# A fused attention and feed-forward kernel: a new order for its first two chunks, and another place in memory for the squares

## The chip, the cores and the metric

One core of a Trainium2 chip runs the whole program in one launch. The metric is device time in microseconds (us); lower is better. PE is TensorE (its matmuls), DVE VectorE, ACT ScalarE, POOL GpSimd, and SP the engine that issues the loads and stores.

## The reference

```python
# attention: 4 batches, 8 heads, 768 positions of 64; windows of 16, blocks of 32
k_sum = k.reshape(B, H, nb, block, D).max(axis=3)       # nb = 24 blocks
v_sum = v.reshape(B, H, nb, block, D).mean(axis=3)
scores_l = scale * q @ k.T, outside |i - j| < window: -1e9
scores_s = scale * einsum('bhsd,bhnd->bhsn', q, k_sum) + log(block)
a = softmax(concatenate([scores_l, scores_s], axis=-1))
attn = a @ concatenate([v, v_sum])                      # -> x, 3072 tokens x 512
# feed-forward: 512 -> 2048 -> 512
h = maximum(x @ w_in, 0.0)
out = h * h @ w_out
```

## The kernel before

The 3072 tokens are 24 tiles of 128 (6 to a batch) and 12 chunks of two tiles. For a tile, `scores` or `scores_kt` makes the scores on PE, `mask_max` (DVE) adds the mask and finds the maximum, `exponentials` (ACT) takes the exponential, `inverse` (DVE) and `norm` (mostly POOL) divide, `turn` (DVE) or `turn_pe` (PE) transposes, and `outputs` (PE) multiplies by the values. `high_x` (ACT) and `low_x` (DVE) split the result into a high and a low part, `xh` and `xl`, from the pool `work`.

The hidden 2048 is 16 slices f of 128. The first layer, `ffn1`, makes per slice 12 matmuls of 256 columns (4 pieces of the 512, each as xh by high weight, xh by low weight, xl by high weight): stationary are 128 columns of the weights `w_sb`, moving is `xh` or `xl`. `squares` takes the ReLU, the square and its high and low parts `gh` and `gl`. The second layer, `ffn2`, makes 6 matmuls of 512 columns per slice: stationary is `gh` or `gl`, moving is `w_sb`. All these operands are fp32r. In all there are 2304 matmuls of the first layer (L390) and 1152 of the second (L434).

Weights arrive as 64-bit words and are split once, at the start, by six steps per slice: HI (`sign_w`, ACT), LO (`round_w`, ACT or DVE), SH (`shift_w`, DVE), AD (`add_w`, POOL), CA (`high_w`, ACT or DVE), SU (`low_w`, DVE or POOL). Slices 0 to 3 do it in halves (.1 is the first layer's, .2 the second's).

Two things set the order. Chunks 2 to 11 are a loop of eight slots (`slot`, `period`), in which attention for the next chunk is laid between. Chunks 0 and 1 with their attention, the split of the weights and all loads of batch 0 follow the list `START` (L42), a token for each step in the order in which every engine takes it: `L:x0` loads value tile 0, `KS` is a maximum of keys, `S` scores, `TT` `mask_max`, `E` `exponentials`, `NR` `inverse`, `N` `norm`, `T` a transpose on PE and `TC` its copy, `SV` and `VC` the value means and their copies, `PK` the copy of the key maxima, `O` `outputs`, `XH`/`XL` the split, `F1.u.j` and `F2.u.j` the two layers of unit u (two slices of one chunk), `RE SQ MU GL` the squares' steps, `EV` an eviction, `Z` zero matmuls that fill PE's time. A letter a, v or p at the end puts a step on ACT, DVE or POOL.

Loads go out on SP, in the list's order; a load whose buffer isn't free holds back those behind it. The means of values (`sum_v0`, L154) need all four `x` loads; `outputs` of tile 0 and 1 need the means. The mask comes with `consts` (L553).

The pool `const` is laid out in the order of its lines, then `big` (18 slots of 8192 bytes for weights), then `work`. Two unnamed tiles, `gap0` (L101, ahead of gh) and `gap` (L110), hold nothing.

Of the kernel before, what the change touches and what calls it, by code (L numbers as in the profile page):

```python
# [43 lines left out]
TT0.2 L:w0.1 TT0.0 L:q2 TT0.3 E0.2 S0.1=23 TT0.1 E0.3 E0.1 E0.0 TT0.6 TT0.4 S1.0=45 TT0.5 S1.1=45 TT0.7 L:w0.2 E0.4
SU2.1p HI0.1 NR0.0 LO0.1v TT1.0 S2.1=01 E0.7 E0.6 SH0.1 TT1.4 TT1.6 E0.5 N0.0p NR0.1 E1.0 S2.0=01 TT1.5 E1.6 L:w1.1
TT1.3 N0.1p T0.0=2 Z2 TT1.1 E1.4 L:q3 T0.1=3 Z3 L:k4 TT1.2 E1.5 TT1.7 LO1.1v E1.7 LO0.2v E1.3 E1.1 TT2.0 TT2.3 TT2.4
L:x0 NR1.1 E1.2 TC0.1a NR1.0 TT2.1 HI0.2 AD0.1 TT2.2 TC0.0v E2.2 L:q4 TT2.5 S3.0=45 TT2.7 HI1.1 N1.1p TT2.6 E2.0 SH0.2
N1.0p S3.1=45 L:x1 L:x3 E2.3 T1.1=3 Z1 E2.4 E2.1 T1.0=2 SH1.1 CA0.1v AD0.2 TC1.0a TT3.6 S4.0=01 TT3.0 E2.6 TT3.7 E3.7
TC1.1v E2.7 TT3.4 TT3.5 SV0 Z5 E2.5 L:x2 E3.6 NR2.0 TT3.1 CA1.1v TT3.3 NR2.1 SV1 TT3.2 S4.1=01 Z1 L:w3.1 E3.4 E3.3
VC0.3a AD1.1 VC0.2v VC0.1a VC0.0v VC1.2a L:w2.2 E3.5 N2.0p L:w3.2 L:w6 VC1.0v HI3.1 VC1.3v SU1.1p VC1.1v N2.1p O0=2  # L50
E3.2 L:w1.2 NR3.1 N3.1v O1=3 XH0 XH1 E3.1 PK5a XL0 XL1 LO3.1a L:w4 E3.0 SH3.1 T2.1=4 VX3v L:q5 CA3.1a T3.1=5 TC3.1a
T2.0=2 SU0.1p AD3.1 F1.0.0=3 F1.0.1 L:k5 NR3.0 TT4.5 TT4.6 TC2.0v CA0.2a TC2.1v HI2.2 F1.1.0=5 VX2a SU0.2v SH2.2 L:w11
HI1.2 RE0v TT4.7 N3.0p T3.0=2 SQ0 SU3.1p L:w7 MU0 LO1.2a SH1.2 CA1.2v CA2.2v O2=4 GL0v AD1.2 TC3.0a TT4.0 XH2 F1.1.1
LO3.2v SU1.2v HI3.2 O3=2 F2.0.0 L:w5 LO2.2v HI4 SH3.2 XL2 XH3 LO4a CA3.2a TT4.1 L:w8 F2.0.1 XL3 AD3.2 E4.0 E4.1 E4.6
S5.1=34 AD2.2 TT4.3 HI7 S5.0=34 TT4.2 HI5 SH4 SU2.2p F1.2.0=2 TT5.4 RE1v SQ1 TT4.4 AD4 L:k6 MU1 F1.2.1 RE2v CA4a TT5.1
L:q6 F1.3.0=0 TT5.7 SU3.2p MU2 F1.3.1 GL1v SU4v LO5a RE3a SQ2 SH5 F2.1.0 L:w9 GL2v TT5.6 F2.1.1 HI6 L:kw2 EV0.0v
F1.4.0=1 EV0.1a SQ3 E4.3 MU3 CA5a HI11 TT5.0 AD5 LO6a SH7 F2.2.0 LO7a LO9v SU5v CA7v SH6 F1.6.0=5 CA6a AD6 L:w10
F2.2.1 F1.4.1 GL3v RE4v HI8 E4.5 SU6v SH8 VT2 L:k7 HI9 L:w12 AD7 E5.0 HI10 L:w13 F2.3.0 TT5.3 KT2 SU7v LO8a F1.6.1
TT5.2 F1.7.0=2 AD8 SQ4 MU4 E5.7 F2.3.1 E4.4 E5.6 GL4v CA8a F1.5.0=0 TT5.5 F1.5.1 LO10a SH10 F2.4.0 F2.4.1 SU8v RE5a
F1.7.1 SQ5 SH9 SH11 HI12 E4.2 HI13 MU5 CA9a F1.12.0=1 RE6v AD9 F1.8.0=3 SQ6 CA11a GL5v MU6 AD10 L:kw3 E4.7 VT3 SU9v  # L60
F2.5.0 F2.5.1 SH13 CA10a NR4.1 RE7v EV1.0v F1.8.1 F1.12.1 E5.2 SU10v GL6p SH12 MU7 EV1.1v LO11a F1.9.0=4 L:w14
F1.13.0=0 RE8a LO12a F2.6.0 AD11 E5.1 F2.6.1 E5.3 HI14 SU11v NR4.0 N4.1p F1.9.1 SQ7 AD12 LO14a E5.4 KT3 MU8 F1.13.1
GL7v L:w15 F2.7.0 LO13a N4.0v SQ8 GL8v CA12a CA13a AD13 LO15a SH14 SU12v RE9a SU13p F2.7.1 E5.5 AD14 MU9 HI15 F2.8.0
F2.8.1 F1.14.0=5 L:kw0 TU4.2 F1.10.0=2 SQ9 F1.10.1 CA14a SH15 SU14v CA15a F1.11.0=3 KT0 AD15 GL9v SU15p F2.9.0 F2.9.1
RE10v SQ10 TU4.1 MU10 NR5.1 GL10v F1.11.1 RE11v SQ11 F2.10.0 MU11 VT0 GL11v F1.15.0=4 NR5.0 RE12a MU12 RE13v F2.10.1
N5.1p SQ12 MU13 F2.11.0 GL12v F2.11.1 EV2.0v L:kw1 F1.14.1 EV2.1v KT1 F1.15.1 L:q7 L:v4 N5.0p SQ13 PK6a GL13p RE15a
TU5.0 F2.12.0 RE14a TU4.0 MU14 TU5.2 S6.1=01 F2.12.1 F2.13.0 F2.13.1 SQ14 MU15 GL14p L:v5 O4=2 F2.14.0 TU5.1 S6.0=01
# [680 lines left out]
```

## Time and profile before

| | us |
|---|---|
| median of 3 runs (622.3 to 624.28) | 622.73 |
| the profiled execution, its own time | 622.01 |
| its span, first to last instruction | 619.9 |
| PE busy | 607.6 |
| DVE busy | 389.8 |
| ACT busy | 267.4 |
| POOL busy | 106.2 |

What lies between the span and the execution's own time is 2.1 us. A matmul's busy time is longer than the distance from its start to the next one's start, since matmuls overlap: for the pace of PE look at starts, not at durations. A time in brackets behind a row is idle time of the engine before it and what ended it.

### The profile page before, as it was taken

The page shows a single profiled execution, that of the slowest core. Times are in us where ns is not written, and L with a number is a line of the kernel's source. Part 1 is how long each engine was busy: PE and PEld are TensorE (multiplying, and loading weights), DVE is VectorE, ACT ScalarE, POOL GpSimd, SP SyncE. Part 2 cuts the span into 40 slices and gives each one's busy share as a digit, 9 for nine tenths or more (in the row PEclk, how much of TensorE's full clock was granted, in tenths as well). Part 3 has the DMA queues.
Part 4 walks back from the last instruction along what each step waited for, and adds up shares of the span by engine and source line. Part 5 has one row for each costly group of instructions (what it writes and reads, how often), then busy time and mean ns, then how long its engine had stood idle before and what let it go on. Part 6 is the DMA issues. An engine that isn't in the chain of part 4 may idle for free.

```text
span 619.9 us, 12969 instructions
## 1 busy us (share of the span) xinstructions
PE 607.6 (98%) x5253; PEld 546.5 (88%) x5253; DVE 389.8 (63%) x1063; ACT 267.4 (43%) x688; POOL 106.2 (17%) x98
## 2 busy tenths in 40 slices
...
GB/s 329 410 413 336 52 136 52 153 193 30 1 9 264 2 2 220 2 2 221 1 2 188 86 1 126 97 1 76 95 2 38 133 1 1 87 1 1 35 1 34
DMA packets 21643, 59.41 MB, mean 96 GB/s; under 512 B 2256, under 2 KB 2256, under 8 KB 20048
## 3 DMA queue, kind: packets, MB, share of 16 engines
...
q14 instruction: 18, 0.15, 0.1%
...
## 4 chain that ended last, share of the span: by engine, by line
PE 93%; DVE 2%; ACT 2%; DMA 2%; SPq 1%; issue 0%; POOL 0%; DVEq 0%; POOLq 0%
PE o_ps L434 42%; PE ph L390 39%; PE s_ps L390 5%; PE ph L360 3%; PE s_ps L277 3%; DMA consts_sb<-in_consts 1%; ACT e_sb L313 1%; DVE w_sb L262 1%; PE s_ps L360 1%; DMA kv<-in_kt 0%; PE o_ps L159 0%; DVE v_sb L126 0%; SPq L180 0%; DVE ksum L188 0%; PE s_ps L339 0%
## 5 line engine op out<-in xcount | busy, mean ns | idle before, releaser
L390 PE MATMUL ph<-xh,w_sb 128*128 128x256 f32 x1360 | 246.8, 282 | 0.5 <-DVE xl L377 0.5
L434 PE MATMUL o_ps<-w_sb,gh 128*128 128x512 f32 x768 | 239.0, 392 | 0.0
L390 PEld LDWEIGHTS ph<-xh,w_sb 128*128 128x128 f32 x1360 | 213.4, 188 | 8.6 <-issue 1.4
L390 PE MATMUL ph<-xl,w_sb 128*128 128x256 f32 x680 | 190.5, 280 | 0.0
L434 PEld LDWEIGHTS o_ps<-w_sb,gh 128*128 128x128 f32 x768 | 137.6, 188 | 25.2 <-issue 0.2
L409 DVE TENSOR_TENSOR ph<-ph,r 128x512 f32<-128x512 f32 x83 | 58.1, 699 | 151.7 <-ACT r L398 150.9
L434 PE MATMUL o_ps<-w_sb,gl 128*128 128x512 f32 x384 | 151.2, 394 | 0.0
L398 ACT ACTIVATE r<-ph 128x512 f32<-128x512 f32 x83 | 49.2, 594 | 199.7 <-PE ph L390 199.7
L390 PEld LDWEIGHTS ph<-xl,w_sb 128*128 128x128 f32 x680 | 128.7, 189 | 0.0
L346 DVE STREAM_TRANSPOSE pT<-e_sb 32x256 f32<-32x256 f32 x240 | 104.6, 436 | 4.1 <-POOL e_sb L333 0.7
L313 ACT ACTIVATE e_sb<-e_sb,nmx 128x120 f32<-128x120 f32 x192 | 73.8, 386 | 68.8 <-DVE nmx L305 68.8
L333 POOL TENSOR_TENSOR e_sb<-e_sb,total 128x480 f32<-128x480 f32 x46 | 46.3, 1014 | 325.8 <-DVE total L327 181.3
L434 PEld LDWEIGHTS o_ps<-w_sb,gl 128*128 128x128 f32 x384 | 72.2, 188 | 15.3
L404 ACT ACTIVATE gh<-r 128x512 fp32r<-128x512 f32 x94 | 59.4, 632 | 11.9 <-DVE r L400 6.8
L412 DVE TENSOR_TENSOR gl<-ph,gh 128x512 fp32r<-128x512 f32 x83 | 57.4, 692 | 8.7 <-DVE ph L409 0.5
L253 POOL TENSOR_TENSOR w_raw<-w_raw 128x1024 int32<-128x1024 int32 (+1 forms) x20 | 34.1, 1712 | 35.6 <-DVE w_raw L248 18.1
L305 DVE CUSTOM_DVE_ANT_0 e_sb<-s_ps,consts_sb 128x120 f32<-128x120 f32 x172 | 38.8, 277 | 0.6 <-DMA consts_sb<-in_consts 0.2
L313 ACT ACTIVATION_READ_ACCUMULATOR e_sb<-e_sb,nmx 128x1 f32 x192 | 36.2, 188 | 0.0
L390 PE MATMUL s_ps<-xh,w_sb 128*128 128x256 f32 x176 | 32.5, 283 | 0.4 <-DVE w_sb L262 0.4
L390 PEld LDWEIGHTS s_ps<-xh,w_sb 128*128 128x128 f32 x176 | 27.5, 188 | 1.6 <-DVE w_sb L262 0.8
L377 DVE TENSOR_TENSOR xl<-ph,xh 128x512 fp32r<-128x512 f32 x19 | 13.1, 691 | 23.3 <-ACT xh L374 23.3
L390 PE MATMUL s_ps<-xl,w_sb 128*128 128x256 f32 x88 | 24.7, 281 | 0.0
...
## 6 DMA issues: line engine op xcount, KB each, us to landing
...
```

The source lines that it names most:

```text
L253: nc.gpsimd.tensor_tensor(out=lo, in0=hi, in1=lo, op=ALU.add)
L305: nc.vector.tensor_tensor_reduce(out=e_sb(g)[:, h, 0:NK], in0=s_ps[g, half][h % 2][:, h // 2, 0:NK], in1=m, scale=-scale, scalar=3.0e38, o ...
L313: nc.scalar.activation(e, e, AF.Exp, bias=nmx[g, half][:, i : i + 1], scale=-1.0, accum_out=sm[g, half][:, i, 0:1])
L333: eng.tensor_mul(out=e, in0=e, in1=sm.pop((g, half)).unsqueeze(2).to_broadcast([P, 4, NK]))
L346: nc.vector.transpose(out=pT[g % 2][j * 32 : j * 32 + 32, :, i * 32 : i * 32 + 32], in_=e_sb(g)[i * 32 : i * 32 + 32, :, j * 32 : j * 32 + ...
L360: nc.tensor.matmul(xp[o : o + 64, h // 2, s * 64 : s * 64 + 64], lhsT=values(g)[:, s, h * 64 : h * 64 + 64], rhs=pT[g % 2][:, h, s * 64 : ...
L390: nc.tensor.matmul(ph, lhsT=w_sb[f][:, w, cc * P : (cc + 1) * P], rhs=x[c][:, cc, :], start=(n == 0), stop=(n == 3 * NC4 - 1))
L398: nc.scalar.activation(r, ph, AF.Relu)
L404: nc.scalar.activation(gh, r, AF.Square)
L409: nc.vector.tensor_mul(out=ph, in0=ph, in1=r)
L412: nc.vector.tensor_sub(out=gl, in0=ph, in1=gh.bitcast(F32))
L434: nc.tensor.matmul(o_ps[c][tt], lhsT=g_[:, ts_], rhs=w_sb[f][:, w, DM:], start=(first and n == 0), stop=(last and n == 2),)
```

## The change

1. `START` is another list for chunks 0 and 1: the order of nearly all steps differs, and some steps change engine (of the half-width low_w steps 5 are on DVE where 2 were, of the half-width round_w steps 3 where 6 were, of the relu steps 7 where 9 were). It has 508 tokens for 510; the zero matmuls are 37 in both.
2. `ON_POOL`, the units whose last subtraction is on POOL: (12, 13) for (6, 13, 14).
3. `gh` and `gl` are allocated first in the pool `const`, behind a gap of 32 words; the second gap has 16 words for 56; and `nmx` has 7 buffers for 6.

The loop over chunks 2 to 11 keeps its instructions and their order.

```diff
-ON_POOL = (6, 13, 14, )
+ON_POOL = (12, 13, )
...
-Z25 L:w2.1 XT L:kv0 LO2.1v L:kv3 L:kv1 L:kv2 KS0 KS3 HI2.1 L:q0 KS1 SH2.1 L:mask S0.0=01 L:q1 KS2 PK4v CA2.1a AD2.1
...
+Z25 L:kv1 L:kv3 XT KS1 L:kv0 L:kv2 L:q0 KS3 KS0 KS2 L:mask S0.0=01 PK4a TT0.0 E0.0 TT0.3 E0.3 L:q1 TT0.2 E0.2 L:w1.1
...
     w_sb = {}
+    const.tile([P, 32], F32, name="gap0")
+    gh_sb = const.tile([P, 4, CT], F32R, name="gh")
+    gl_sb = const.tile([P, 4, CT], F32R, name="gl")
     consts_sb = const.tile([P, 3 * NK + P + 8 * 32], F32, name="consts_sb")
...
-    const.tile([P, 56], F32, name="gap0")
-    gh_sb = const.tile([P, 4, CT], F32R, name="gh")
-    gl_sb = const.tile([P, 4, CT], F32R, name="gl")
-
...
-    const.tile([P, 56], F32, name="gap")
+    const.tile([P, 16], F32, name="gap")
...
-            nmx[g, half] = work.tile([P, 4], F32, name="nmx", tag="nmx", bufs=6)
+            nmx[g, half] = work.tile([P, 4], F32, name="nmx", tag="nmx", bufs=7)
```

Distances in bytes within a partition, from the allocation of the two programs (weights: the first of the 18 slots):

| | before | changed |
|---|---|---|
| xh minus weights | 147,872 | 147,904 |
| gh minus weights | -8,768 | -55,360 |
| xh minus gh | 156,640 | 203,264 |

The first grows by 32, since the seventh `nmx` takes 32 bytes ahead of xh. Modulo 512 the three were 416, 448 and 480 and are 448, 448 and 0.

How the list moves instructions, at two places. On SP, the loads from the start of the program to the last value load of batch 0 (`in_w`: weights, `in_x`: values, `in_kt` and `in_k`: keys, `in_q`: queries). Before:

```order
L226 DMA w_raw<-in_w 128x512
L180 DMA kv<-in_kt 128x768 x4
L130 DMA q_sb_75<-in_q 128x512
L553 DMA consts_sb<-in_consts 128x744
L130 DMA q_sb_76<-in_q 128x512
L226 DMA w_raw<-in_w 128x512
L130 DMA q_sb_77<-in_q 128x512
L226 DMA w_raw<-in_w 128x512 x2
L130 DMA q_sb_75<-in_q 128x512
L133 DMA k_sb_71<-in_k 128x768
L150 DMA v_sb_73<-in_x 128x1024
L130 DMA q_sb_76<-in_q 128x512
L150 DMA v_sb_74<-in_x 128x1024
L150 DMA v_x<-in_x 128x1024 x2
```

and now:

```order
L179 DMA kv<-in_kt 128x768 x4
L129 DMA q_sb_78<-in_q 128x512
L552 DMA consts_sb<-in_consts 128x744
L129 DMA q_sb_79<-in_q 128x512
L225 DMA w_raw<-in_w 128x512
L129 DMA q_sb_80<-in_q 128x512
L225 DMA w_raw<-in_w 128x512
L129 DMA q_sb_78<-in_q 128x512
L149 DMA v_sb_76<-in_x 128x1024
L149 DMA v_sb_77<-in_x 128x1024
L225 DMA w_raw<-in_w 128x512
L149 DMA v_x<-in_x 128x1024 x2
```

One half weight load (512 KB) has left the place ahead of the consts, and one half weight load, one k and one q load (512, 384 and 256 KB) have left the place ahead of the last value load.

On PE, the end of the list, at the change from chunk 1 to chunk 2 (L360, now L359, is `outputs` of tiles 4 and 5, L277 the scores of the tiles after them). Before:

```order
L360 MATMUL s_ps<-pT_80,v_sb_73 64x64 x16
L434 MATMUL o_ps<-w_sb,gh 128x512 x2
L434 MATMUL o_ps<-w_sb,gl 128x512
L434 MATMUL o_ps<-w_sb,gh 128x512 x2
L434 MATMUL o_ps<-w_sb,gl 128x512
L277 MATMUL s_ps<-k_sb_71,q_sb_75 64x120 x8
L360 MATMUL s_ps<-pT_81,v_sb_74 64x64 x16
L434 MATMUL o_ps<-w_sb,gh 128x512 x2
L434 MATMUL o_ps<-w_sb,gl 128x512
L434 MATMUL o_ps<-w_sb,gh 128x512 x2
L434 MATMUL o_ps<-w_sb,gl 128x512
L277 MATMUL s_ps<-k_sb_72,q_sb_76 64x120 x16
```

and now:

```order
L433 MATMUL o_ps<-w_sb,gh 128x512 x2
L433 MATMUL o_ps<-w_sb,gl 128x512
L359 MATMUL ph<-pT_83,v_sb_76 64x64 x16
L359 MATMUL ph<-pT_84,v_sb_77 64x64 x16
L389 MATMUL ph<-xh,w_sb 128x256 x2
L389 MATMUL ph<-xl,w_sb 128x256
```

Chunk 2's first matmul (L389) now stands right behind the `outputs` that make its xh and xl, where second-layer matmuls and scores stood between.

## Rows read from the trace of the kernel before

**Rows 1.** The page: its first line, and busy time, share of the span and number of instructions of each engine.

```profile
span 619.9 us, 12969 instructions
PE 607.6 (98%) x5253; PEld 546.5 (88%) x5253; DVE 389.8 (63%) x1063; ACT 267.4 (43%) x688; POOL 106.2 (17%) x98
```

**Rows 2.** Busy time by stretch: from:to, length, then busy us (and instructions) of PE, PEld, DVE, ACT and POOL, the granted clock of PE, the busy share of the DMA engines, GB/s.

```profile
0.00:25.00 25.00, 19.32 (x356) 15.66 (x356) 18.30 (x91) 15.77 (x62) 13.88 (x22) 1.00 0.94 359
25.00:50.00 25.00, 23.72 (x331) 21.11 (x330) 22.21 (x65) 21.88 (x47) 16.00 (x13) 1.00 1.02 413
50.00:75.00 25.00, 24.62 (x160) 22.19 (x159) 22.70 (x38) 22.64 (x37) 10.06 (x7) 1.00 0.47 183
75.00:100.00 25.00, 25.00 (x167) 22.94 (x166) 24.47 (x31) 18.38 (x31) 17.61 (x9) 1.00 0.34 116
100.00:125.00 25.00, 24.24 (x179) 20.81 (x178) 19.78 (x40) 6.74 (x12) 8.20 (x6) 1.00 0.32 95
300.00:350.00 50.00, 50.00 (x428) 45.47 (x427) 29.05 (x81) 18.67 (x55) 3.95 (x4) 1.00 0.25 85
```

**Rows 3.** The chain that ended last, its longest pieces in the steady part: start, us, what, count.

```profile
173.50 3.02 PE ph L390 x24
...
222.33 3.02 PE ph L390 x24
...
299.34 2.85 PE ph L390 x24
302.19 2.76 PE o_ps L434 x12
304.95 2.85 PE ph L390 x24
```

**Rows 4.** PE in order of time at the start: start, us, instruction, count. L566 are zero matmuls, L159 the value means, L360 `outputs`, L390 the first layer.

```profile
23.54 0.41 PE L159 MATMUL o_ps<-v_sb,consts_sb 128*32 128x128 f32 x4 [0.37 <-issue]
23.89 1.36 PE L566 MATMUL o_ps<-zero 128*128 128x512 f32 x5
25.17 1.08 PE L159 MATMUL o_ps<-v_x,consts_sb 128*32 128x128 f32 x32
28.04 1.27 PE L360 MATMUL s_ps<-pT,v_sb 128*64 128x64 f32 x36 [0.80 <-DVE v_sb L126]
32.23 0.50 PE L390 MATMUL s_ps<-xh,w_sb 128*128 128x256 f32 x2
```

**Rows 5.** The chain of the first 46 us: the load of the consts, the exponentials on ACT, and the first copy of the value means.

```profile
3.88 6.62 DMA consts_sb<-in_consts
11.00 2.03 ACT e_sb L313 x10
13.03 0.58 ACT w_raw L237
13.61 3.98 ACT e_sb L313 x21
26.32 0.37 ACT v_sb L126
```

**Rows 6.** The value loads: from SP's order of time the issue of the last two, from the view of line L150 the time from issue to landing of the four, and the GB/s of the stretch from 3 to 25 us in 40 slices.

```profile
13.47 1.94 SPq L150 DMA_DIRECT2D v_x<-in_x  x2
DMA to landing us min/median/max: 7.8/9.0/9.7
GB/s 272 289 361 413 374 380 425 408 404 409 429 404 409 439 406 376 421 398 425 432 298 328 384 393 430 404 408 406 406 439 380 425 410 417 372 417 395 432 395 417
```

**Rows 7.** PE around 63 and 68 us in order of time: its two waits for weights.

```profile
63.14 0.28 PE L390 MATMUL s_ps<-xh,w_sb 128*128 128x256 f32 x1
63.63 0.39 PE L390 MATMUL s_ps<-xh,w_sb 128*128 128x256 f32 x1 [0.20 <-DVE w_sb L262]
...
67.86 0.28 PE L390 MATMUL s_ps<-xh,w_sb 128*128 128x256 f32 x1
68.32 0.39 PE L390 MATMUL s_ps<-xh,w_sb 128*128 128x256 f32 x1 [0.17 <-DVE w_sb L262]
```

**Rows 8.** Groups of DVE instructions to 131 us, shapes apart: busy us, mean ns. L262 is the half-width low_w on DVE, L242 the half-width round_w.

```profile
L262 DVE TENSOR_TENSOR w_sb<-w_raw,w_sb 128x512 fp32r<-128x512 f32 x2 | 2.4, 1196 | 0.0
L242 DVE TENSOR_SCALAR w_raw<-w_raw 128x512 int32<-128x512 uint32 x6 | 2.8, 487 | 4.5 <-DMA w_raw<-in_w 4.5
```

**Rows 9.** The wait at 117 us: a key load in the chain, DVE's maximum behind it, PE's scores behind that.

```profile
113.94 3.06 DMA kv<-in_kt
117.02 0.95 DVE L188 TENSOR_REDUCE ksum<-kv 128x24 f32<-128x768 f32 x1 [2.88 <-DMA kv<-in_kt]
118.41 0.64 PE L277 MATMUL s_ps<-k_sb,q_sb 64*64 64x120 f32 x16 [0.76 <-ACT k_sb L126]
```

**Rows 10.** PE in order of time at two changes of chunk: at 129 us from the list to the loop, and at 562 us, the one change in the loop that has no scores between `outputs` and the next first layer.

```profile
129.23 1.05 PE L277 MATMUL s_ps<-k_sb,q_sb 64*64 64x120 f32 x32
130.21 0.50 PE L390 MATMUL ph<-xh,w_sb 128*128 128x256 f32 x2
...
560.23 2.08 PE L360 MATMUL ph<-pT,v_sb 128*64 128x64 f32 x64
562.79 0.50 PE L390 MATMUL ph<-xh,w_sb 128*128 128x256 f32 x2 [0.48 <-DVE xl L377]
```

**Rows 11.** Zero matmuls at 4.3 us, one group of 18 in order of time: start, us from the first start to the last end. Each lasts 0.38 us.

```profile
4.33 4.12 PE L566 MATMUL o_ps<-zero 128*128 128x512 f32 x18
```

More of the change, by code (lines that the diff above doesn't have):

```diff
@@ L42 @@
 START = """
-Z25 L:w2.1 XT L:kv0 LO2.1v L:kv3 L:kv1 L:kv2 KS0 KS3 HI2.1 L:q0 KS1 SH2.1 L:mask S0.0=01 L:q1 KS2 PK4v CA2.1a AD2.1
[L44 to L67, printed above, removed]
@@ L68 @@
-PK7v SQ15 XH4 O5=3 F2.14.1 XL4 XH5 GL15v XL5 S7.0=23 S7.1=23 VT1
+Z25 L:kv1 L:kv3 XT KS1 L:kv0 L:kv2 L:q0 KS3 KS0 KS2 L:mask S0.0=01 PK4a TT0.0 E0.0 TT0.3 E0.3 L:q1 TT0.2 E0.2 L:w1.1
+TT0.1 S0.1=23 L:q2 TT0.6 L:w0.1 E0.1 TT0.4 E0.6 L:q3 S1.0=45 S1.1=45 TT0.5 HI1.1 S2.1=01 PK5v NR0.0 LO1.1v N0.0p TT1.3
+TT1.0 E0.5 E0.4 TT1.5 E1.3 TT0.7 SH1.1 L:x0 S2.0=01 TT1.7 TT1.6 E0.7 TT1.1 NR0.1 TT1.4 E1.0 T0.0=2 Z6 AD1.1 TC0.0v
+E1.5 HI0.1 L:x1 E1.7 N0.1p TT1.2 T0.1=3 E1.6 LO0.1v E1.2 S3.1=24 SH0.1 CA0.1v L:w2.1 E1.1 TT2.1 TT2.4 E1.4 E2.1 L:x2
@@ new lines @@
+NR1.1 TT2.2 L:x3 SV0 Z3 L:k4 TT2.5 AD0.1 NR1.0 N1.1p T1.1=5 Z3 SV1 CA1.1a E2.5 N1.0p TT2.6 E2.4 TT2.7 E2.6 TT2.0
+TC0.1v L:q4 TT3.7 HI2.1 SH2.1 CA2.1v LO2.1a L:w3.1 TT3.5 E2.7 TT2.3 NR2.1 AD2.1 T1.0=3 E2.0 L:w0.2 E2.3 VC0.0v VC0.1v
+VC0.3v S4.1=01 E2.2 VC0.2a SU2.1p TC1.0a NR2.0 VC1.0a S3.0=24 O0=3 VC1.1a TC1.1v VC1.2a TT3.0 VC1.3a N2.0p TT3.1 N2.1p
+HI3.1 TT3.3 TT3.4 TT3.6 XH0 O1=5 TT3.2 S4.0=01 E3.6 XH1 SU1.1v XL0 L:w1.2 T2.1=2 T2.0=4 XL1 L:w4 E3.3 HI0.2 LO3.1v
+E3.0 SH3.1 E3.2 L:k5 SU0.1p SH0.2 E3.4 AD3.1 TC2.1v TC2.0v CA3.1a VX2v F1.0.0=3 L:w2.2 LO0.2a F1.0.1 E3.5 SU3.1v
@@ new lines @@
+F1.1.0=5 E3.7 RE0v L:w5 AD0.2 O2=2 F1.1.1 NR3.1 VX3a E3.1 N3.1p SQ0 CA0.2a LO1.2a MU0 T3.1=4 HI1.2 L:q6 XH2 NR3.0 L:q5
+GL0v N3.0p SU0.2v T3.0=3 TC3.0a L:w3.2 SH1.2 TC3.1v L:w7 AD1.2 F2.0.0 TT4.2 L:w6 CA1.2a TT4.0 XL2 O3=3 RE1v HI2.2
+SH2.2 LO2.2a XH3 TT4.5 L:w9 L:w8 HI4 XL3 CA2.2a SQ1 L:kw3 SU1.2p S5.1=42 LO3.2a S5.0=42 L:k7 F2.0.1 TT4.4 AD2.2 LO4v
+F1.2.0=3 SH4 TT4.7 MU1 HI3.2 GL1v F1.2.1 TT4.3 HI5 TT4.1 TT5.4 CA4a F1.3.0=5 TT4.6 L:v4 AD4 SU2.2v LO5a SH3.2 F2.1.0
+TT5.0 CA3.2v RE2v F1.3.1 TT5.6 L:w11 L:w10 LO7a AD3.2 SU3.2v SU4v SQ2 SH5 F2.1.1 AD5 MU2 HI6 F1.4.0=0 F1.6.0=1 RE3v
```

12 lines of the change are left out of this document (added).

## Prediction, made before the changed kernel was run

> **What bounds the kernel now.** I read the page first. PE is busy 607.6 us of a span of 619.9 [rows 1], the other engines far less, so the time is PE's work plus the few stretches in which PE has nothing to do. The view by stretch says where those are: PE is busy 19.32 us of the first 25 and 23.72 of the next, then nearly all the time [rows 2]. It also says that the granted clock stays at 1.00, the 2.4 GHz level, and that DVE, at 22.21, 22.70 and 24.47 us of 25, is close to full from 25 to 100 us. The third view is the chain that ended last: from 173.50 to 222.33 us it is PE alone, one period of 48.8 us, with 24 first-layer matmuls in 2.85 us and 12 second-layer ones in 2.76 [rows 3]. That is 118.7 ns and 230 ns for one. At 2.4 GHz 256 columns take 106.7 ns and 512 take 213.3, so each carries an excess of 12.0 and 16.7 ns.
>
> So there are two places where this change can act: the front, up to about 130 us, where the list decides when PE starts on the feed-forward and whether it is fed, and the pace of the 3456 large matmuls, if that pace depends on where their operands lie.
>
> The profiled execution took 622.01 us, 2.1 more than its span, and stands 0.7 below the median of 622.73. I make the sum on the execution and move the result by that 0.7. A difference under 0.3% (1.9 us) counts as none.
>
> **The new list, at the front.** PE's first first-layer matmul starts at 32.23 us [rows 4]. It waits for `outputs` of tiles 0 and 1, which wait for the value means. The second half of the means starts on PE at 25.17, behind five zero matmuls that started at 23.89 [rows 4]. The last value load lands at 24.1 (issued at 14.4, the end of the row from 13.47 less half of its 1.94, plus 9.7) [rows 6]. So loads and PE's order together set 25.17.
>
> In the changed list 1152 KB less stand ahead of the last value load. The loads run at about 410 GB/s [rows 6], so 1152 KB (1.18 MB) are 2.9 us: the last value load lands at about 21.2. Also 512 KB less stand ahead of the consts, 1.3 us: they land at 9.2 for 10.5 (3.88 plus 6.62) [rows 5], and the exponentials start that much earlier. Will the exponentials be in time? In the trace the first 31 instructions on ACT end at 17.6, with one weight step of 0.58 among them [rows 5]. With 1.3 less and a second weight step they end at 16.9. Behind them come `inverse`, `norm`, a transpose and three zeros, some 2.5 us by their rows, so 19.4: before the loads. From the second half of the means on, the chain to the first layer (copies, two `outputs`, the split) has the same steps on both sides, so I carry the shift through. Its lower end is the 1.3 us of the consts, if the softmax rules after all; its upper end is 25.17 less 21.2, or 4.0, if the zeros no longer stand in the way. I take **2.9 us earlier**, the bytes alone.
>
> **What DVE makes of it.** If PE starts 2.9 us earlier, DVE has to deliver the split weights and squares 2.9 us earlier, and it is nearly full. Two waits show that it is only just in time now: PE loses 0.37 us at 63.14 and 0.34 at 67.86 beyond its pace, both on `low_w` from DVE [rows 7]. In the changed order 15 weight instructions stand on DVE ahead of the fourth `low_x`, where 20 stood; at 0.49 us for a half-width one [rows 8] that is 2.4 us, and the consts give 1.3, so DVE leads by 3.7 early on. Over the whole list it gets more work: three half-width `low_w` from POOL, 1.20 us each, less three `round_w` at 0.49 that go to ACT [rows 8], 2.1 us in all; the other exchanges pair off (two relu leave, two transpose copies come). The lead covers the 2.9 and leaves 0.8 of the 2.1. The remaining 1.3 falls mostly into the stretch from 100 us on, where DVE is busy 19.78 of 25 [rows 2]. Ends: both waits vanish (0.7 faster), or all 2.1 turn into waits of PE. I take **0.2 slower**. What POOL loses (three `low_w`) costs nothing: it is 17% busy [rows 1]. The shorter `ON_POOL` is one subtraction more on DVE and one eviction less, so nothing.
>
> **The wait at 117 us.** PE waits 0.76 us for scores whose key maximum waits for a key load that lands at 117.0 [rows 9]. In the changed list all four loads of this kind are issued before the first output store, so this one is long there. **0.8 faster**; ends 0 and 0.9.
>
> **The change to the loop.** Before, scores lie between the last `outputs` and chunk 2's first layer, and there is no wait [rows 10]. Now the first layer stands right behind `outputs`. The loop has that pattern once, at 562 us, and PE waits 0.48 us for `low_x` there [rows 10]. DVE is less loaded at that point than earlier, so I take the same: **0.5 slower**; ends 0.4 and 1.0.
>
> Sum: -2.9 + 0.2 - 0.8 + 0.5 = **-3.0 us**. The execution would take 619.0, and the median 619.7. With the ends it runs from -5.2 (-4.0 - 0.7 - 0.9 + 0.4) to +1.8 (-1.3 + 2.1 + 0 + 1.0).
>
> **The new places in memory.** No instruction is added by them. The first layer's moving operand lies 448 bytes after its weights modulo 512 where it lay 416; the second layer's distance is 448 on both sides. The trace has one layout only, so it can't price this. Bounds: the nearest row below is the zero matmuls, (4.12 - 0.38) / 17 or 220 ns each [rows 11], an excess of 6.7 (they read one element over and over). If the first layer's 12.0 fell to that, 2304 times 5.3 ns is 12.2 us less. The nearest row above is the second layer's excess of 16.7 [rows 3]: 2304 times 4.7 ns is 10.8 us more. Within the trace the weights' slices move by 512 bytes and xh and xl by 1024 from matmul to matmul, and the pace of a group of 24 is 2.85 us each time [rows 3], whatever the slot; the only row for the first layer is its own, so I take **0**.
>
> The Trainium skill, TensorE: Matmul & The Clock Gate, "Step-by-step: what each phase is for", says that PE reads moving operand and weights over two independent ports, so that loading the next weights takes no bandwidth from the running matmul. By that rule the distances are worth nothing and the sum stays at -3.0; no row here shows whether it holds.
>
> **Rivals.**
> *DVE takes the front gain back* (0.20). For it: 69.4 us busy of 75 between 25 and 100, and two waits already. Against it: the lead of 3.7 us. It decides once `low_w` or a square comes more than 1 us late after 40 us. All of the 2.1 us as waits leave a gain of about 1.1: 621.6, no difference that can be told.
> *The layout makes the first layer faster* (0.15). For it: an excess of 12.0 ns where zero matmuls have 6.7. Against it: no dependence on the slot. Half of the way, 2.65 ns, is 6.1 us: 613.6.
> *The layout makes the first layer slower* (0.15). Same place, other sign: the weight load of the next matmul then collides with the moving reads more often. It eats the gain from 1.3 ns per matmul on (3.0 us over 2304) and the kernel is slower by over 0.3% from 2.1 ns on. At the full 4.7 ns it is 630.5, at half 625.1.
> That the list doesn't start PE earlier at all is the lower end above, with 1.3 at the front.
>
> The Trainium skill, same page, "Back-to-back issue gap", gives N/2.4 + 2.5 ns for one isolated matmul, an estimate of 109 ns for 256 columns. The trace disagrees, with 118.7; were the layout all that keeps PE from that pace, 2304 times 9.5 ns would be 22 us, which I hold too unlikely for a case of its own.
>
> **How the numbers follow.** Forecast case (-3.0, layout without effect): 0.50, all of it faster. DVE rival: 0.20, within 0.3%. Layout faster: 0.15, all faster. Layout slower: 0.15, of which 0.13 slower and 0.02 within 0.3%. So faster 0.65, same 0.22, slower 0.13. The forecast case alone reaches from 617.5 (622.7 less 5.2) to 620.8, where a gain can still be told; the upper ends belong to the DVE rival. With part of both layout cases, and at most 2 in 10 left out, the range is 614.0 to 624.0.
>
> **What would show it.** Right: the last value load lands near 21 us and the first first-layer matmul starts near 29.3; no key load in the chain near 110 us; a wait of about 0.5 us ahead of chunk 2; a period of 48.8 us. DVE rival: more waits of PE on DVE's `low_w`, squares or `low_x` between 40 and 100 us than 0.7 us in all. Layout: groups of 24 first-layer matmuls away from 2.85 us, through the whole loop. The prediction is wrong if that group changes by more than 0.05 us, or if the start of the first layer moves by less than 1.3 us.

## The result

The changed kernel takes 613.14 us (median of 4 runs, 612.71 to 613.37) where the kernel before takes 622.61 in the same job (622.3 to 624.28): a ratio of 0.9842, 95% interval 0.9823 to 0.986. The forecast was 619.7, with a range from 614.0 to 624.0. The profiled execution took 612.71 us, 9.3 less than the one of before; its span is 9.1 less.

The page of the changed kernel, its first line and the busy times, answers to [rows 1].

```profile
span 610.8 us, 12985 instructions
PE 599.2 (98%) x5253; PEld 539.2 (88%) x5253; DVE 387.1 (63%) x1061; ACT 269.7 (44%) x694; POOL 101.9 (17%) x94
```

PE does the same 5253 matmuls in 8.4 us less of busy time. Busy time by stretch (columns as in [rows 2]) says where it is not: the granted clock is 1.00 in both, and PE's idle time of the first 75 us falls by 0.9 us only, from 7.3 to 6.4.

```profile
0.00:25.00 25.00, 20.66 (x345) 16.50 (x346) 15.94 (x83) 14.11 (x56) 12.81 (x20) 1.00 0.90 324
25.00:50.00 25.00, 23.77 (x345) 21.69 (x346) 23.59 (x71) 23.27 (x49) 14.34 (x12) 1.00 1.02 409
50.00:75.00 25.00, 24.14 (x164) 21.68 (x162) 23.75 (x36) 21.86 (x32) 12.55 (x6) 1.00 0.71 247
...
300.00:350.00 50.00, 50.00 (x430) 45.36 (x429) 31.29 (x89) 19.06 (x55) 3.64 (x4) 1.00 0.25 85
```

The chain that ended last says where it is (start, us, what, count):

```profile
93.20 2.83 PE ph L389 x24
...
162.91 2.75 PE ph L389 x24
165.66 2.75 PE o_ps L433 x12
172.22 2.94 PE ph L389 x24
...
220.19 2.94 PE ph L389 x24
```

A group of 24 first-layer matmuls takes 2.75 us in the loop where it took 2.85 [rows 3], and a period, from 172.22 to 220.19, 47.97 us instead of 48.83. From chunk 2's first matmul to the end of the span the changed kernel needs 481.6 us (610.8 less 129.19), the kernel before 489.7 (619.9 less 130.21 [rows 10]). **So 8.1 of the 9.1 us come from the loop, whose instructions did not change, and 1.0 from the list.** At 93 us, still inside the list, the same 24 matmuls take 2.83: in the list, the first layer is hardly faster.

The starts of PE's matmuls show two patterns. In order of time, three rows of the list and three of the loop (the third matmul of each triple, on xl, is left out):

```profile
86.03 0.40 PE L389 MATMUL s_ps<-xh,w_sb 128*128 128x256 f32 x2
...
86.38 0.40 PE L389 MATMUL s_ps<-xh,w_sb 128*128 128x256 f32 x2
...
86.74 0.40 PE L389 MATMUL s_ps<-xh,w_sb 128*128 128x256 f32 x2
...
131.18 0.39 PE L389 MATMUL ph<-xh,w_sb 128*128 128x256 f32 x2
...
131.51 0.39 PE L389 MATMUL ph<-xh,w_sb 128*128 128x256 f32 x2
...
131.85 0.39 PE L389 MATMUL ph<-xh,w_sb 128*128 128x256 f32 x2
```

By these rows, which are rounded to 0.01 us, three matmuls take some 0.355 us in the list and 0.335 in the loop. Taken from all starts, the slow pattern is 117.8 ns a matmul and the fast one 113.3; in the loop the first five distances of a group are mostly 117 to 123 ns and the rest 113.3, so the mean there is 114.4. Before, the mean was 118.4. In the changed kernel a group stays in its pattern to its end. Of the 384 first-layer matmuls of the list 288 stand in groups of the slow pattern; of the loop's 1920 only one group of 24 does.

### The profile page after: what moved, and what is told of

The parts are those of the page before. It is cut to its first block, busy times and chain, and to the rows that moved or that the text cites. A ratio compares the mean times of both kernels' runs of the same rounds, so it can differ in the third digit from the quotient of the medians.

```text
span 610.8 us, 12985 instructions
## 1 busy us (share of the span) xinstructions
PE 599.2 (98%) x5253; PEld 539.2 (88%) x5253; DVE 387.1 (63%) x1061; ACT 269.7 (44%) x694; POOL 101.9 (17%) x94
## 4 chain that ended last, share of the span: by engine, by line
PE 88%; DVE 6%; DMA 2%; ACT 1%; issue 1%; SPq 0%; DVEq 0%
PE o_ps L433 41%; PE ph L389 38%; PE ph L359 3%; PE s_ps L276 3%; PE s_ps L389 2%; DVE w_sb L261 2%; DMA v_x<-in_x 2%; PE o_ps L565 1%; DVE w_raw L247 1%; DMA kv<-in_vt 1%; DVE xl L376 0%; DVE e_sb L304 0%; ACT xh L373 0%; DVE gl L411 0%; DVE vsum L192 0%
## 5 line engine op out<-in xcount | busy, mean ns | idle before, releaser
L389 PE MATMUL ph<-xh,w_sb 128*128 128x256 f32 x1376 | 242.3, 279 | 1.2 <-ACT xh L373 0.7
L389 PEld LDWEIGHTS ph<-xh,w_sb 128*128 128x128 f32 x1376 | 213.3, 188 | 9.2 <-issue 1.4
L389 PE MATMUL ph<-xl,w_sb 128*128 128x256 f32 x688 | 190.7, 277 | 0.2 <-DVE xl L376 0.2
L408 DVE TENSOR_TENSOR ph<-ph,r 128x512 f32<-128x512 f32 x86 | 60.1, 699 | 143.3 <-ACT r L397 142.4
L389 PEld LDWEIGHTS ph<-xl,w_sb 128*128 128x128 f32 x688 | 129.4, 188 | 0.4 <-DVE xl L376 0.4
L332 POOL TENSOR_TENSOR e_sb<-e_sb,total 128x480 f32<-128x480 f32 x46 | 45.0, 988 | 322.0 <-DVE total L326 180.4
L403 ACT ACTIVATE gh<-r 128x512 fp32r<-128x512 f32 x96 | 60.7, 632 | 14.6 <-PE o_ps L433 10.5
L411 DVE TENSOR_TENSOR gl<-ph,gh 128x512 fp32r<-128x512 f32 x86 | 59.5, 692 | 9.2 <-DVE ph L408 0.5
L376 DVE TENSOR_TENSOR xl<-ph,xh 128x512 fp32r<-128x512 f32 x21 | 14.5, 692 | 24.8 <-ACT xh L373 24.8
L389 PE MATMUL s_ps<-xh,w_sb 128*128 128x256 f32 x160 | 29.0, 281 | 0.1
L389 PEld LDWEIGHTS s_ps<-xh,w_sb 128*128 128x128 f32 x160 | 25.0, 188 | 1.1 <-DVE w_sb L261 0.4
L373 ACT CAST xh<-ph 128x512 fp32r<-128x512 f32 x21 | 12.3, 586 | 30.8 <-PE ph L359 30.8
```

The costliest lines, as they stand in the source:

```text
L332: eng.tensor_mul(out=e, in0=e, in1=sm.pop((g, half)).unsqueeze(2).to_broadcast([P, 4, NK]))
L389: nc.tensor.matmul(ph, lhsT=w_sb[f][:, w, cc * P : (cc + 1) * P], rhs=x[c][:, cc, :], start=(n == 0), stop=(n == 3 * NC4 - 1))
L403: nc.scalar.activation(gh, r, AF.Square)
L408: nc.vector.tensor_mul(out=ph, in0=ph, in1=r)
L411: nc.vector.tensor_sub(out=gl, in0=ph, in1=gh.bitcast(F32))
```

## Experiments

The time of each run is compared with runs of the kernel before on the same chip and in the same job (their medians lie between 622.0 and 622.6); times of different jobs stand side by side in the table. "First layer" and "second layer" are mean distances from one start to the next inside groups, from 175 to 560 us. Distances in memory are modulo 512 bytes: xh behind the weights, then the weights behind gh (448 for "gh minus weights" is 64 here).

| run | xh, weights | first layer, ns | second layer, ns | period, us | time, us |
|---|---|---|---|---|---|
| before | 416, 64 | 118.4 | 230.0 | 48.83 | 622.61 |
| changed | 448, 64 | 114.4 | 228.9 | 47.96 | 613.14 |
| e1 | 448, 64 | 114.4 | 228.8 | 47.96 | 612.62 |
| e2 | 416, 64 | 118.4 | 230.0 | 48.83 | 621.07 |
| e3 | 416, 32 | 118.9 | 233.2 | 49.21 | 626.58 |
| e4 | 448, 32 | 117.3 | 233.4 | 48.95 | 623.64 |
| s1 | 0, 128 | 119.7 | 231.6 | 49.19 | 625.31 |
| s2 | 64, 0 | 117.9 | 229.9 | 48.69 | 621.73 |
| s3 | 128, 256 | 119.6 | 230.2 | 49.07 | 623.22 |
| s4 | 384, 448 | 118.5 | 232.7 | 49.11 | 624.16 |
| g1 | 448, 64 | 114.4 | 228.8 | 47.96 | 612.65 |
| g2 | 448, 32 | 117.3 | 233.4 | 48.95 | 623.49 |
| g3 | 448, 0 | 117.3 | 226.8 | 48.32 | 614.49 |
| h1 | 480, 64 | 118.2 | 229.2 | 48.74 | 620.66 |
| h2 | 448, 96 | 114.4 | 233.3 | 48.39 | 615.85 |

e1, e2 and g3 were timed in rounds; e3, e4, the four s, g1, g2, h1 and h2 have one time each, and their periods carry the argument.

### Layout or list: e1 and e2

e1, on the kernel before:

```diff
-    const.tile([P, 56], F32, name="gap0")
+    const.tile([P, 40], F32, name="gap0")
-            nmx[g, half] = work.tile([P, 4], F32, name="nmx", tag="nmx", bufs=6)
+            nmx[g, half] = work.tile([P, 4], F32, name="nmx", tag="nmx", bufs=7)
```

> The kernel before with its own list and with gh and gl in their old place; only a seventh nmx buffer (32 bytes) and 16 words less in gap0, so that xh lies 448 bytes behind the weights modulo 512 instead of 416, and everything else as in the changed kernel modulo 512. Distance theory: a group of 24 first-layer matmuls takes 2.75 us instead of 2.85, a period of the loop 47.97 us instead of 48.83, and the time is 8 to 9 us below that of the kernel before, 613.5 to 614.8. List theory (the new list is what made the gain, over the whole program): pace as before, 622.6. Theory that gh's move to the front of the pool matters: pace as before, 622.6.

e2, on the changed kernel: `nmx` with `bufs=6`.

> The changed kernel with 6 nmx buffers instead of 7, so that xh lies 416 bytes behind the weights again; the new list and gh's new place stay. Distance theory: groups of 24 at 2.85 us, period 48.8 us, and what is left is the list's gain of about 1 us at chunk 2's start: 621.0 to 621.8. List theory or theory of gh's place: the pace stays at 2.75 us and the time near 613.

Measured: e1 612.62 us for 622.46, ratio 0.983 (0.9785 to 0.9875); e2 621.07, ratio 0.9961 (0.994 to 0.9982). The chain of e1:

```profile
183.26 2.75 PE ph L390 x24
```

and of e2:

```profile
184.24 2.85 PE ph L389 x24
```

What follows: 32 bytes between weights and xh, without any other part of the change, give 9.8 us (about 1 to 2 more than expected), and taking them away takes all but 1.4. That they come with a seventh `nmx` buffer is not the cause: e4 and g2 below have it too and gain nothing. gh's new place in the pool is not needed. The list gives 1.4 us at the old distance, and nothing that can be told at the new one (612.62 without it, 613.14 with it, in another job). The two gains do not add; the two traces show a reason. At the new distance 372 of the old list's 384 first-layer matmuls stand in fast groups, and 96 of the new list's. The difference, 276 matmuls at 4.5 ns, is 1.2 us, about the list's gain of 1.0.

### Distance or place: e3, e4 and g1

e3 is the kernel before with `gap` at 48 words for 56; e4 is e3 with `nmx` at 7 buffers; g1 is the changed kernel with `gap0` at 24 words for 32.

> The kernel before with the second gap 8 words shorter: weights and xh both 32 bytes lower, so that their distance stays 416, but xh now starts at a multiple of 64 bytes and the weights do not. If the distance between xh and the weights decides: groups of 24 first-layer matmuls stay at 2.85 us. If the place of xh by itself decides: 2.75 us. If the place of the weights by itself decides: another pace than both. The second layer's weights lie 32 bytes behind gh instead of 64: if such a distance decides there too, the 228.9 ns from start to start of its matmuls change.

> The run before this one with a seventh nmx buffer: the distance is 448, while xh starts at an odd multiple of 32 bytes, as in the kernel before. If the distance decides: groups of 24 at 2.75 us, and about 8 us less than the kernel before for the first layer alone. If the place of xh by itself decides: 2.85 us.

> The changed kernel with the first gap 8 words shorter: gh, weights and xh all 32 bytes lower, none at a multiple of 64 now, all distances kept (448, 64, 0). Theory (distances alone decide): loop as in the changed kernel, 113.3 ns in nearly all groups, 47.96 us a period. Rival (the place by itself decides which pattern the first layer falls into): mostly 117.8 ns, near 48.8 us a period.

The chain of e3:

```profile
180.32 2.86 PE ph L390 x24
183.18 2.79 PE o_ps L434 x12
```

of e4:

```profile
185.33 2.83 PE ph L390 x24
188.16 2.80 PE o_ps L434 x12
```

and of g1:

```profile
183.50 2.75 PE ph L389 x24
```

g1 settles the place: everything 32 bytes lower, and pace and time are those of the changed kernel (but for chunk 2, whose seven groups run in the slow pattern in g1's trace; 73 of the loop's 80 are fast). e3 fits: xh at a multiple of 64 does not help at 416. e4 was a miss for the plain distance theory: 448 and yet 2.83 us, the slow pattern of the changed kernel's list (1680 of 1920 matmuls of its loop; the 240 others are the first group of each chunk, behind attention work). What e4 has beside 448 is a second layer at 32.

### What picks the pattern: g2, g3 and h2

g2 is the changed kernel with `gap0` at 40 and `gap` at 8 words, so that of the two layers' operands only gh and gl move. g3 and h2 are f2 (below) without `gap`, and with `gap` at 24 words.

> The changed kernel with gh and gl alone 32 bytes higher: weights 32 behind gh instead of 64, xh still 448 behind the weights, weights and xh in the same places. Theory (how the second layer's group ends decides the pattern in which the next first-layer group runs): second layer at 233 ns and the first layer mostly at 117.8 ns in the loop, though its own operands have not moved. Rival (the first layer's own operands decide): first layer stays at 113.3 ns, only the second layer's 233.

> The changed kernel with the shift_w moved behind the low square (610.57 us) and without the second gap: weights 0 behind gh instead of 64, first layer at 448. In the run with 0 and a first layer of 64 the second layer settled at 226 to 227 ns after a slow start of its group. If that holds and the first layer keeps its fast pattern, 1152 matmuls at about 1.5 ns are 1.7 us less, 608.9. If the first layer falls into the slow pattern: 2304 at 4.5 ns at most, 610 to 621. Theory of the exits: either is possible, the same pace as now is not expected.

> The same kernel, with the second gap 8 words longer instead: weights 96 behind gh instead of 64, first layer still at 448. Theory (the pair alone, and the second layer's group ends decide the first layer's pattern): second layer away from 228.8 ns, between the 233 of 32 and the 231.6 of 128, and the first layer mostly at 117.8. Rival (a range): 228.8 and 114.3 as now, 610.6 us.

The chain of g2:

```profile
185.25 2.83 PE ph L389 x24
188.08 2.80 PE o_ps L433 x12
```

of g3:

```profile
182.13 2.83 PE ph L388 x24
184.96 2.72 PE o_ps L432 x12
```

and of h2:

```profile
182.65 2.75 PE ph L389 x24
185.40 2.80 PE o_ps L433 x12
```

g2 leaves the first layer's operands where they were and moves the second layer's stationary ones by 32 bytes: 70 of the loop's 80 first-layer groups fall into the slow pattern, and pace and period equal e4's. So the pattern of a first-layer group depends on the second-layer group in front of it too, not on its own operands alone. The starts show how a state may keep itself up: in the changed kernel (64) a second-layer group whose last distance, to the first layer's first start, is 226 or 227 ns is followed by a slow group, one with 230 or 231 by a fast one, with one exception in 83; and behind a slow group the second layer begins with 235 ns, behind a fast one with 227 or 228. Each state would so reproduce itself until other work breaks it, which is a reading of the starts and not tested. At 0 (g3) the last distance is 226 or 227 each time in the loop: a second layer 2.0 ns faster than f2's, and a slow first layer. At 96 (h2) it is 231: a second layer 4.5 ns slower, and every loop group fast. At 32 (g2), however, it is 230 or 231 as well, and slow groups follow: that last distance alone is not the rule, and what at the end of a group decides stays open. The third distance, from gh to xh, is not the rule either: it is 0 modulo 512 in f2 and 32 in h2, both fast, and 32 in h1 below, which is slow. h2 was a half miss: I expected the slow pattern there. Time follows: g3 614.49 (ratio 0.9853, 0.9817 to 0.989), h2 615.85, both behind f2's 610.57, from which they differ in that distance alone.

### Other distances: s1 to s4, and h1

All with the changed kernel's list, h1 with f2's edit. s1 has a tile of 16 words that holds nothing ahead of xh and `gap` at 32 words; s2 32 words and no `gap`; s3 48 words, no `gap`, `sm` ahead of gh; s4 5 buffers of `nmx`, `sm` and one `ksum` ahead of gh; h1 8 words ahead of xh.

> The changed kernel with a tile of 16 words that holds nothing ahead of xh and the second gap 16 words longer: xh lies 0 bytes behind the weights modulo 512 (448 in the changed kernel), the weights 128 behind gh (64). Theory that the distance of the two operands of a layer sets that layer's pace, each by its own: both paces move away from the changed kernel's 114.3 ns (first layer, 113.3 in its fast pattern and 117.8 in its slow one) and 228.8 ns (second layer), independently; by the four pairs known so far (first layer 416: 118.6, 448: 114.3; second layer 32: 233.3, 64: 228.8) I guess first layer 113 to 122, second layer 220 to 233. Rival, that 448 is good only because it is the same distance as gh's to the weights: first layer back to 118.6 or more here. No effect beyond the 32-byte step: both stay.

> The changed kernel with 32 words ahead of xh and no second gap: xh 64 bytes behind the weights modulo 512, weights 0 behind gh. Distance theory: the second layer leaves 228.8 ns, upward to 233 or more if it goes on as from 64 to 32; the first layer between 113 and 122 by its own distance. Rival (same distance for both layers): first layer slow, 118.6 or more.

> The changed kernel with 48 words ahead of xh, no second gap and the 256 bytes of sm ahead of gh: xh 128 bytes behind the weights modulo 512, weights 256 behind gh, the farthest from 0. Distance theory with a collision that grows as the two reads come close: the second layer is at its fastest here, toward the 220 ns of the zero matmuls. Rival (same distance for both): first layer 118.6 or more.

> The changed kernel with 5 nmx buffers and with sm and one ksum ahead of gh: xh 384 bytes behind the weights modulo 512 (64 below 448 where before was 32 below), weights 448 behind gh. Distance theory: if 448 is better than 416 because it is a multiple of 64 bytes, the first layer is near 114 ns at 384 too; if because it is nearer to 512, it is at 118.6 or more. Second layer: moving 64 bytes ahead of stationary, which is the first layer's own distance in the changed kernel; if one law holds for both layers, its excess over 213.3 ns is at most the first layer's 6.7 to 7.6 ns plus what the longer row adds, some 220 to 222 ns.

> The changed kernel with the shift_w moved behind the low square (610.57 us) and 8 words ahead of xh: xh 480 bytes behind the weights instead of 448, all else kept. Theory (a fast pattern exists at this pair alone): first layer between 117 and 120 ns, as at 416 and 0. Rival (a range, from 448 up to some value below 512): 113.3 to 114.3 as now.

Paces are in the table. Of seven distances for the first layer (0, 64, 128, 384, 416, 448, 480) only 448 shows the fast pattern. But only 416, 448 and 480 were tried with 64 at the second layer. The four s runs move both distances, and 448 is itself mostly slow with 32 or 0 at the second layer, so they don't show what 0, 64, 128 and 384 give at 64. s2 missed for the second layer, which at 0 left 228.8 ns for 229.9 and not for 233 or more. s3 was a miss: the farthest distance is not the fastest for the second layer. s4 was one too: 448 at the second layer, the first layer's good distance, gives 232.7 ns, so the two layers do not follow one law, and "the same distance for both" is not what counts (h2 is fast without it: its xh lies 448 behind the weights, its gh 416). h1's chain, one step above 448:

```profile
184.52 2.84 PE ph L390 x24
```

### Where the front's gain went: f1, f2, f3, f4 and g4

f1 moves loads in the list, ahead of or right behind the fourth query load:

```diff
-... E0.6 L:q3 S1.0=45 ... L:x0 ... L:x1 ... L:w2.1 ... L:x2 ... L:x3 SV0 ...
+... E0.6 L:x0 L:x1 L:q3 L:x2 L:x3 L:w2.1 S1.0=45 ... SV0 ...
```

> The changed kernel with its value loads taken out from behind the fourth query load: the first two go out ahead of it, the last two right behind it, and the half weight load that stood between them behind those. In the changed kernel SP waits from 6.16 to 11.13 us with that query load, whose buffer is still in use, and the last value load lands at 23.19. Theory (the predicted 2.9 us shrank to 1.0 because the queue was held, not because bytes count for nothing): the loads go on without a gap, the last value load lands near 20.1 us, and the first first-layer matmul starts 1 to 3 us before 31.18. Rival (the softmax chain or PE's order sets the front, not the loads): the loads land earlier and the first layer starts within 0.5 us of 31.18. Either way the time gains less than the start, since DVE is nearly full from 25 to 100 us: 611 to 613.3.

SP of the changed kernel in order of time:

```profile
5.51 0.61 SPq L225 DMA_DIRECT2D w_raw<-in_w  x1
11.13 0.33 SPq L129 DMA_DIRECT2D q_sb<-in_q  x1
```

and of f1, and PE's start there:

```profile
6.49 1.46 SPq L149 DMA_DIRECT2D v_sb<-in_x  x2
10.14 0.33 SPq L129 DMA_DIRECT2D q_sb<-in_q  x1
10.51 0.94 SPq L149 DMA_DIRECT2D v_x<-in_x  x2
...
30.02 0.49 PE L389 MATMUL s_ps<-xh,w_sb 128*128 128x256 f32 x2
```

The last value load lands at 19.94 (23.19 in the changed kernel), 3.3 us earlier, and the first layer starts 1.2 us earlier, at 30.02. Not all of the 1.2 is the edit's: PE's zero matmuls at the start take 7.62 us in f1 and 8.61 in the changed kernel's trace, and the queue hangs on them (see the front, below). With zeros of like length the edit gives 0.5 to 1.2 us: 30.02 against 30.49 in f2, 30.86 in g1 and 31.22 in s1 (7.48 to 7.57 us), and 30.65 in g4 below against the changed kernel's 31.18 (8.61 both). So both theories hold a part: the held queue kept the values back, and once they are early, ACT waits 1.83 us for the weight load that now stands behind them and PE 1.29 us for a copy on ACT. Time: 612.33, ratio 0.9839 (0.9824 to 0.9854), not told apart from the changed kernel's 0.9842.

f2 moves one shift on DVE:

```diff
-SH9 SU8v E4.5 L:q7 F1.7.0=5 SH12 LO12a F1.5.1 TT5.3 E4.4 F1.7.1 F2.4.0 TT5.5 RE5a MU5 SQ5 E4.3 GL5v CA9a AD9 LO11a
+SH9 SU8v E4.5 L:q7 F1.7.0=5 LO12a F1.5.1 TT5.3 E4.4 F1.7.1 F2.4.0 TT5.5 RE5a MU5 SQ5 E4.3 GL5v SH12 CA9a AD9 LO11a
```

> The changed kernel with one shift_w on DVE (slice 12, 70.94 us, 2.39 us long where others of its size take 0.69) moved behind the low part of square 5, for which PE waits 1.15 us at 73.82. Theory (that wait is made by this shift, which drags on beside an add_w on POOL): the wait is gone or under 0.3 us. Theory of two patterns: PE's first-layer matmuls go on after it at 113.3 ns from start to start, where in the changed kernel they fall back to 117.8 from 77.6 to 114 us, so the stretch up to the scores at 114 us is shorter by the wait and by some 130 matmuls at 4.5 ns, 1.1 + 0.6 = 1.7 us, and the time is near 611.5. Rival (the slow pattern at the front comes from the place in the program, not from what went before): the pace stays at 117.8 from 77 us on, 612.0. Rival (another DVE step is late next): no change, 613.1.

DVE, POOL and PE of the changed kernel in order of time:

```profile
69.21 0.68 DVE L247 TENSOR_SCALAR w_raw<-w_raw 128x1024 int32<-128x1024 int32 x1
...
70.94 2.39 DVE L247 TENSOR_SCALAR w_raw<-w_raw 128x1024 int32<-128x1024 int32 x1
...
74.44 0.69 DVE L411 TENSOR_TENSOR gl<-s_ps,gh 128x512 fp32r<-128x512 f32 x1
...
70.02 2.75 POOL L252 TENSOR_TENSOR w_raw<-w_raw 128x1024 int32<-128x1024 int32 x1 [1.02 <-ACT r L397]
...
73.59 0.62 PE L433 MATMUL o_ps<-w_sb,gh 128*128 128x512 f32 x2
75.19 0.50 PE L433 MATMUL o_ps<-w_sb,gl 128*128 128x512 f32 x1 [0.98 <-DVE gl L411]
```

The shift that takes 0.68 us at 69.21 takes 2.39 at 70.94, while POOL's add runs to 72.77, and the low square behind it comes 1.15 us too late for PE. In f2:

```profile
71.17 0.69 DVE L411 TENSOR_TENSOR gl<-s_ps,gh 128x512 fp32r<-128x512 f32 x1
71.78 0.69 DVE L247 TENSOR_SCALAR w_raw<-w_raw 128x1024 int32<-128x1024 int32 x1
...
72.88 0.62 PE L433 MATMUL o_ps<-w_sb,gh 128*128 128x512 f32 x2
73.34 0.39 PE L433 MATMUL o_ps<-w_sb,gl 128*128 128x512 f32 x1
```

The wait is gone, and the groups behind it stay in the fast pattern (252 of the list's 384 matmuls stand in fast groups, 96 in the changed kernel). f2 takes 610.57 us, ratio 0.9814 (0.9797 to 0.983): faster than the kernel before, and below the changed kernel's 613.14, which is of another job. From 41 to 168 us its trace gains 1.9 us on the changed kernel's: 1.15 for the wait plus 156 matmuls at 4.5 ns, 0.7.

The second part is not the edit's alone, for the wait turns the pattern over, whichever it is. In the changed kernel and g1 (0.98 and 0.71 us idle there) the groups are fast ahead of it and slow behind it, in f1 and f3 (0.39 and 0.38) slow ahead and fast behind; in f2, f4 and g4, without the wait, the pattern ahead goes on. The changed kernel and f3 have the same list up to there and opposite patterns, so the 0.7 us hang on the pattern that the execution was in.

f3 gives the end of the list the old order (`O4 F2.14.0 O5 F2.14.1`, scores of tile 7 last); f4 has f1, f2 and f3 together. In both, the outputs of tile 5 are written over the bank from which the low part of square 15 is taken afterwards, so that slice's low part is other data; kind and number of instructions stay.

> The changed kernel with the last units of the list in the order that the kernel before has at the change to the loop: a piece of the second layer between the outputs of tiles 4 and 5, another behind them, and the scores of tile 7 last. In the changed kernel PE loses 0.85 us at 128.29 and 0.39 at 129.41 before and in chunk 2's first layer. Theory (predicted 0.5, measured 1.2, for want of work between outputs and the first layer): at most 0.3 us is left, the first second-period outputs start 0.9 to 1.2 us earlier than 168.34. Rival (low_x itself is late, whatever stands between): within 0.3 us of 168.34.

> The three edits of the runs before this one together. If their gains add: 613.1 less 1 to 2 (value loads), 1.1 to 1.7 (shift) and 1 (boundary), 608.5 to 610. If DVE sets the front: 610.5 to 612. Two patterns: the pace of the first layer in the front is 113.3 or 117.8 by group, whichever it falls into, which by itself moves the sum by up to 1.7 us (379 matmuls at 4.5 ns).

f3 starts chunk 2's first layer like this:

```profile
125.50 0.69 PE L359 MATMUL ph<-pT,v_sb 128*64 128x64 f32 x16
126.47 0.69 PE L359 MATMUL ph<-pT,v_sb 128*64 128x64 f32 x16 [0.28 <-DVE pT L345]
...
129.66 0.51 PE L389 MATMUL ph<-xh,w_sb 128*128 128x256 f32 x2
```

The waits for xh and xl are gone, but PE now waits 0.28 us for a transposed tile and changes six times between kinds of matmul, at about 0.1 us each. Against the changed kernel it gains 1.07 us from 41 to 168 us (its outputs stand 1.04 later at the first and 0.03 earlier at the second), and two other things give nearly that much: 144 more matmuls in the fast pattern in this stretch (0.65) and 0.6 less at the wait by 74 us, less 0.29 more at 58. That leaves 0.1 for the boundary, where 0.9 to 1.2 were expected; f3 took 612.62, f4 611.13 (ratio 0.982, 0.9805 to 0.9834).

> The two edits of the value loads and of the shift_w together, on the changed kernel. They gave 0.8 and 2.5 us by themselves. If they add: 609.8. If DVE takes back what the earlier start gives: 610.5 or more.

g4, f1's and f2's edits on the changed kernel, takes 610.77 (0.9798, 0.9765 to 0.983): the early values add nothing to f2. Its first layer starts at 30.65 us and 372 of the list's 384 matmuls stand in fast groups; by 168 us it stands where f2 stands (165.93 and 165.73).

## Why the prediction was wrong

**The new places in memory, priced at 0: this step failed.** The loop gave 8.1 us. My bounds, -12.2 to +10.8, held it; the value I took between them did not. I argued that the pace is the same for all slots, so places don't matter. But the slots are 8192 bytes apart and the pieces 512 and 1024: all have the same distance modulo 512, and a row in which a quantity never varies says nothing about it. "The layout makes the first layer faster" had a chance of 0.15 at 2.65 ns a matmul; it was 4.0 (118.4 to 114.4), and 1.1 of the second layer, whose own distance had not changed, came with it. For the loop's 1920 and 960 matmuls that is 7.7 + 1.1, some 8.7 us by the means, 8.1 by the starts, which also carry the boundary. The Trainium skill (TensorE: Matmul & The Clock Gate, "Step-by-step: what each phase is for") gives moving operand and weights two independent ports, and I drew from it that distances are worth nothing. That does not hold here: e1 changes the distance of the two operands by 32 bytes and takes 4.0 ns off a matmul. Whether the ports have a part in it no run shows.

**The list at the front, -2.9: mis-sized.** The first first-layer matmul starts at 31.18 us for 32.23 [rows 4], 1.05 earlier. The chain of the changed kernel's start says why:

```profile
1.18 8.61 PE o_ps L565 x25
9.79 1.32 PE s_ps L292 x64
...
13.59 9.60 DMA v_x<-in_x
...
```

The value loads stand behind a query load that SP holds until the scores of tile 0 have read its buffer, at 11.13 us; in the trace of before that same load goes out at 11.04. So the last value load's issue moves only from 14.4 to 13.59, and its landing from 24.17 to 23.19. The bytes that left the queue were 2.9 us, but the queue ran short instead: the last weight load of it lands at 14.29, then one query load at 15.81 and the first values at 18.12. I counted bytes ahead and not the issue that holds them, though I had read SP's order. The chain behind the landing was carried through rightly: 8.06 us from landing to first layer before, 7.99 after.

A part of the shortfall is this execution's and not the list's. With the new list, the scores of tile 0 follow the 25 zero matmuls at the start nearly without a wait, so the query load hangs on how long the zeros take, and that differs. In the trace of before and in f2, whose list is the changed kernel's up to 70 us:

```profile
1.18 7.27 PE L566 MATMUL o_ps<-zero 128*128 128x512 f32 x25 [1.18 <-DVE zero L116]
...
1.18 7.57 PE L565 MATMUL o_ps<-zero 128*128 128x512 f32 x25 [1.18 <-DVE zero L115]
...
10.19 0.33 SPq L129 DMA_DIRECT2D q_sb<-in_q  x1
...
30.49 0.48 PE L389 MATMUL s_ps<-xh,w_sb 128*128 128x256 f32 x2
```

The changed kernel's zeros take 8.61 us: their starts lie 427 ns apart up to 7.2 us, which is 512 columns at 1.2 GHz, and 219 apart from there; in f2 the change comes at 5.1 us. (The views give a granted clock of 1.00 for this stretch all the same.) So in f2 the load goes out 0.9 us earlier, and the first layer starts 1.74 us ahead of the kernel before's and not 1.05. In thirteen traces with this start of the list the first layer starts between 30.49 and 33.11, median 31.18; three of the four latest (g2, h1 and s2) have a granted clock of 0.50 for 3.4 to 6.8 us from 24 us on. In four traces of the old list it starts between 32.12 and 32.28, with zeros of 7.18 to 8.68 us. So the new list's front gains 1.05 us at the median and 1.74 at most; the predicted 2.9 is in no trace.

**DVE's give-back, +0.2:** too low. The waits at 63 and 68 us [rows 7], 0.7 in all, are gone, but a new one of 1.15 stands at 74 (f2). What no term of mine had is the slow pattern in the list: it costs nothing against the kernel before (117.8 ns for 118.4), but keeps back 1.3 us that the fast one would have given (288 matmuls at 4.5 ns).

**The wait at 117 us, -0.8:** came as forecast. PE does not wait there, and no key load stands in the chain now; it is PE from 109.96 to 128.53.

**The change to the loop, +0.5:** the wait came, and its size was near the upper end, 1.0. PE waits for xh and xl:

```profile
126.42 2.08 PE L359 MATMUL ph<-pT,v_sb 128*64 128x64 f32 x64
129.19 0.50 PE L389 MATMUL ph<-xh,w_sb 128*128 128x256 f32 x2 [0.69 <-ACT xh L373]
129.92 0.38 PE L389 MATMUL ph<-xl,w_sb 128*128 128x256 f32 x1 [0.23 <-DVE xl L376]
```

0.92 us in two waits, where the loop's own such place has 0.48 [rows 10]. But f3 shows that the old order is hardly better here, since its changes of kind cost about as much; the term priced the new order's wait and put the old one's changes at nothing.

**What would show it** was named rightly: a group away from 2.85 us by more than 0.05, and a first layer that moves by less than 1.3 us. Both came.
